# A pair sum moved ahead of the first product, a bank swapped, a transpose moved behind an addition, and a copy cut in two, in the first unit of a fused attention and feed-forward kernel

## The chip, the cores and the metric

The kernel runs on one core of one Trainium2 chip. The metric is the device time of one execution in microseconds (us); lower is better. The core's engines work side by side, each through its own list of instructions in order: TensorE (PE in the profile, with its weight loads as PEld), VectorE (DVE), ScalarE (ACT), GpSimd (POOL) and SyncE (SP), which issues most of the DMA transfers. They wait for each other on semaphores. What an engine's instruction waits for holds up everything behind it on that engine.

## The reference

Attention over keys and values that are averaged in groups of 8 rows, for 8 batches of 8 heads, 576 rows of 64; then a feed-forward layer with a sine activation on the 4608 rows of 512:

```python
k_p = k.reshape(B, H, Sp, pool, D).mean(axis=3)          # Sp = 576 / 8 = 72
v_p = v.reshape(B, H, Sp, pool, D).mean(axis=3)
scores = scale * np.matmul(q, k_p.transpose(0, 1, 3, 2))
attn = np.exp(scores - np.max(scores, axis=-1, keepdims=True))
attn = attn / (np.sum(attn, axis=-1, keepdims=True) + 1e-09)
attn_out = np.matmul(attn, v_p)
x = attn_out.transpose(0, 2, 1, 3).reshape(B * S, H * D)
h = x @ w_in                                             # 512 -> 2048
s = np.sin(alpha * h)
g = h + s * s / (alpha + 1e-09)
out = g @ w_out                                          # 2048 -> 512
```

All inputs and the output are float32.

## The kernel before

The feed-forward part is the bulk of the work on PE. Rows are taken in units of 512 (`self.NU` = 9 units). Both large products use a scheme with seven block products in the place of eight: sums and differences of blocks of `w_in` (`combine_w_in`, L678) and of `x` (`sums_of_x`, L803) go into seven products, and their results are combined in PSUM and on DVE. PE's time in the first half is the first of these products (`product` in `hidden`, L841), in the second half the second (L1321).

`hidden(u)` (L813) walks through 28 slots for a unit: four groups J of 256 columns, and in each group seven slots, one per product, in the order 1, 5, 6, 2, 7, 3, 4. Around the products it puts the copies between PSUM banks on ACT (`copy`, L817), the additions on DVE (`add`, L816; L1043), and the sines and squares on ACT (L991, L998). The attention of the next batch is cut into pieces that `carry(u)` (L1162) hangs into these slots: `at(slot, f, ...)` appends a piece, and the pieces of a slot are issued by `extras()` in the order in which they were appended. `product` in a slot comes after the slot's extras. So the order on each engine is written out by hand; no scheduler moves anything.

Batch 0 has no unit before it to hide in. `first_batch` (L1068) runs its attention at the start as far as is needed for the first product, and the rest of it lies in the first slots of unit 0: the pair sum of v for the second half of the heads (`sum_v_rows`, L203: matmuls L210 with a matrix of ones and zeros, copied by ACT at L211), the last 64 queries (`rest_q`, L401: transposes L406, copy L407), the transposes of the weights of heads 4 to 7 (`a_head(1)`, L467: L473 and L481), their products with v (`values`, L557: L563, L565; then ACT's L534 into `x` and DVE's differences L574), and the scores of the last 64 rows (`score(4)`: L348, then L355 and L356 on DVE).

PSUM has eight banks. The products of `hidden` rotate through banks 0 to 4 (`bank`), attention pieces through 5 to 7 (`abank`, which steps `self.aturn`), or they name a bank (`psum(shape, i)`). In `first_batch` the last call, `A.values((0, 1), (5, 6), 2, 0)`, leaves its results in banks 5 and 6; ACT reads them into `x` (L534, in four pieces), then DVE reads them for the differences (L574). Product 1 of group 0 needs the first two pieces of L534.

For batch 1, `load_q(1)` brings q into the tile `q0` by rows and heads. `pairs_q` (L87, copies L97 on ACT, one per tile of rows, five in all) reorders it into the tile `q1`. Then `q_t` (L279) transposes `q1` on PE (L287) and writes the turned q into a tile that is again `q0` (L288; DVE for tiles 0 and 1, ACT for 2 to 4): the tile that the raw q occupies. `k_t` (L271) does the same with the pooled keys (L276 on PE, L277 on DVE). `two_scores(0)` in slot 5 takes both (L315 on PE, shifts L338 and L339 on DVE).

The softmax weights of batch 1 follow in slots 9 to 19: `exp` on ACT (L364), `norm` (L370, L371 on DVE, L372 on POOL), `turn(i)` (32x32 transposes on DVE, L498 and L501 to L508) and `move` (DMA, L518), for four tiles i. `turn(2)` is in slot 17, `turn(3)` in slot 19. Slot 19 begins with the DVE addition L816 that reads the bank of product 7, and product 4 in slot 20 adds into that bank.

Of the kernel before, what the change touches and what calls it, by code (L numbers as in the profile page):

```python
# [19 lines left out]
P = 128  # L20
# [20 lines left out]
class Kernel:  # L41
# [214 lines left out]
    def attention(self, b):  # L256

        nc, D, H, Sp, NP, S = self.nc, self.D, self.H, self.Sp, self.NP, self.S
# [142 lines left out]
        def rest_q():  # L401

            rest = self.q_rest
            ps = self.abank([P, NP, 64])
            for hp in range(NP):
                nc.tensor.transpose(ps[:, hp], rest[:, 2 * hp:2 * hp + 2, :].rearrange("p h d -> p (h d)"), self.ident[:64, :64])  # L406
            nc.scalar.copy(out=self.qt_tiles(b)[:, 4, :, :64], in_=ps)  # L407
# [189 lines left out]
        def all_values():  # L597
# [26 lines left out]
            for hp in hps:  # L624
                to_x(ps[hp].rearrange("p (t j) -> p j t", t=4), hp, 0, 512)
            to_x(rest, slice(0, 4), 512, 64)

        return SimpleNamespace(**{f.__name__: f for f in (k_t, q_t, products, score, two_scores, two_shifts, exp, norm, new_a, turn, move, values, values_rest, all_values,
                                                          k_head, k_last, q_head, rest_q, products_head, soft_shift, soft_exp, norm_head, norm_rest, a_head, a_rest)})


# [436 lines left out]
    def first_batch(self):  # L1068

        nc = self.nc  # L1070
        self.att = [self.attention(b) for b in range(self.B)]
        A = self.att[0]

        far = [self.home(i, [P, 4 * POOL * self.D]) for i in (1, 2)]
        h = [self.hp.tile([P, 4 * POOL * self.D], F32, name="h") for _ in range(2)]
        self.k_rows = far[0][:].rearrange("p (h t d) -> p h t d", h=self.H, t=4)
        self.k_sums = far[1][:, 0:1024].rearrange("p (h u d) -> p h u d", h=self.H, u=2)
        self.new_q(0)
        self.load_alpha(self.hp.tile([P, P], F32, name="s", bufs=1)[:])
        self.load_q_heads(0, 0, 2, nc.scalar)  # L1080
        add_k = [self.load_k_heads(0, nc.sync, nc.vector)]
        add_rest = self.load_k_rest(h[1][:, 576:832], far[1][:, 1024:1152])
        one = self.sm.tile([P, 1], F32, name="one")
        nc.scalar.activation(out=one[:], in_=self.ident[:, 0:1], func=AF.Sqrt)

        def fill(n):

            for _ in range(n):
                nc.tensor.matmul(self.psum([P, 4, P], 4), self.full[:], self.full[:].unsqueeze(1).to_broadcast([P, 4, P]), start=True, stop=True)
        fill(5)  # L1090
        self.turn_alpha()
        refine = self.root()
        nc.scalar.activation(out=one[:], in_=one[:], func=AF.Exp)
        add_k[0]()
        tr = self.new_tr()
        nc.gpsimd.memset(tr[:, 2048:], 0.0)
        self.a0 = tr[:, 0:2048].rearrange("p (t j s k) -> p t j s k", t=4, j=4, s=2)
        self.z0 = tr[:, 2048:2560].rearrange("p (t hp x k) -> p t hp x k", t=4, hp=4, x=4)
        self.kb2 = h[1][:, 0:self.H * self.Sp].rearrange("p (h k) -> p h k", h=self.H)
        self.a4 = self.last[:64, 0:512].rearrange("p (j s k) -> p j s k", j=4, s=2)  # L1100
        self.z4 = self.last[:64, 512:640].rearrange("p (hp x k) -> p hp x k", hp=4, x=4)
        nc.gpsimd.memset(self.z4, 0.0)
        for hp in range(1, 4):
            add_k.append(self.load_k_heads(hp, nc.sync, nc.vector if hp < 2 else nc.gpsimd))
            if hp < 3:
                self.load_q_heads(0, 2 * hp, 2 * hp + 2)
        self.load_v_rows(0, h[0][:], self.tp.tile([P, self.DM], F32, name="p5")[:])
        self.load_q_heads(0, 6, 8)
        self.load_w_in()
        self.load_w_in_part(0)  # L1110
        self.q_rest = self.A[3][:64, 0, 512:1024].rearrange("p (h d) -> p h d", h=self.H)
        A.new_a()
        fill(4)
        A.k_head(0)
        add_rest()
        A.q_head(0)
        A.k_last()
        for f in add_k[1:]:
            f()
        fill(1)  # L1120
        A.products_head(0)
        A.q_head(1)
        A.k_head(1)
        A.soft_shift(0)
        A.soft_exp(0)
        fill(1)
        A.products_head(1)
        A.k_head(2)
        A.q_head(2)
        A.soft_shift(1)  # L1130
        A.soft_exp(1)
        A.norm_head(0, nc.gpsimd)
        A.norm_head(1, nc.vector)
        fill(2)
        A.products_head(2)
        self.sum_v_rest(0, 0)
        self.sum_v_rows(0, 0, 3)
        A.k_head(3)
        A.q_head(3)
        A.soft_shift(2)  # L1140
        A.a_head(0, (1, 7, 0), (0,))
        self.add_v_rows(1)
        self.combine_w_in(0, (0,), nc.gpsimd)
        A.products_head(3)
        A.a_head(0, (1, 7, 0), (1,))
        A.soft_exp(2)
        A.soft_shift(3)
        A.norm_head(2, nc.gpsimd)
        A.soft_exp(3)
        A.norm_head(3, nc.vector)  # L1150
        A.values((0, 1), (5, 6), 2, 0)
        self.combine_w_in(0, (1,))
        self.combine_w_in(0, (2, 3), nc.gpsimd)
        self.refine = refine
        self.load_q_rest(0, self.q_rest)
        for e in range(2):
            self.load_k(1, e)
            self.pool_k[e]()
        self.load_q(1)
        self.load_w_in_part(1)  # L1160

    def carry(self, u):  # L1162
# [3 lines left out]
        at = lambda slot, f, *a: x[slot].append(lambda: f(*a))  # L1166
        last = self.B - 1
        b = u + 1
        if u == 0:
            A0, A = self.att[:2]  # L1170
            at(1, self.sum_v_rows, 0, 1, 2, 1)
            at(1, A0.rest_q)
            at(1, A0.a_head, 1, (5, 7, 2))
            at(1, self.refine)
            at(2, A0.values, (2, 3), (2, 1), 1, 1)
            at(2, A0.score, 4)
            at(2, self.sums_of_x, 0, 2)
            at(2, self.sums_of_x, 0, 3)
            at(2, self.load_w_in_part, 2)
            at(2, self.load_w_in_part, 3)  # L1180
            at(2, self.pairs_q, 1, range(5))
            at(4, self.combine_w_in, 1, (0, 1, 2, 3), self.nc.gpsimd)
            at(4, A.q_t, 0, self.nc.vector.tensor_copy)
            at(4, A.q_t, 1, self.nc.vector.tensor_copy)
            at(4, A.k_t)
            at(7, self.load_v, 1)
            at(7, lambda: self.pool_v())
            for i in range(2):
                at((5, 10)[i], A.two_scores, i)
            at(13, A.two_shifts)  # L1190
            for i in range(2, 5):
                at(5 + i, A.q_t, i)
            at(9, A0.exp, 4)
            for i in range(4):
                at((9, 9, 15, 15)[i], A.exp, i)
                at((10, 10, 16, 16)[i], A.norm, i)
                at((13, 13, 17, 19)[i], A.turn, i)
            at(8, self.combine_w_in, 2, (0, 1, 2, 3), self.nc.gpsimd)
            at(13, A0.norm_rest)
            at(17, self.combine_w_in, 3, (0, 1), self.nc.gpsimd)  # L1200
            at(17, self.combine_w_in, 3, (2, 3), self.nc.gpsimd)
            at(23, A0.a_rest)
            at(24, lambda: A0.values_rest((5, 6, 7, (self.turn + 1) % 5)))
            for r in (32, 96):
                at(3, self.nc.gpsimd.memset, self.aM[r:r + 32, :, 704:736], 0.0)
            at(19, A.move, range(3))
            at(20, A.move, (3,), nc.scalar, (0,))
            at(21, A.move, (3,), nc.scalar, (1,))
            at(26, A.all_values)
            at(9, self.load_q, 2)  # L1210
            at(23, self.inner_w_in)
            for e in range(2):
                at(12, self.load_k, 2, e)
                at(17, lambda e=e: self.pool_k[e]())
            at(27, self.att[2].k_t)
            turn = 23
        else:
            at(0, self.sums_of_x, u, 2)
            at(0, self.sums_of_x, u, 3)
        if 0 < u < last:  # L1220
            A = self.att[b]
# [366 lines left out]
```

## Time and profile before

| | |
|---|---|
| median of 3 runs | 905.33 us (903.86 to 905.96) |
| the profiled execution | 904.85 us |
| its span, first to last instruction | 903.1 us |
| PE busy | 894.6 us, 99% |
| DVE busy | 678.1 us, 75% |
| ACT busy | 448.4 us, 50% |
| POOL busy | 211.2 us, 23% |
| mean granted PE clock | 1.00 |

The page gives the busy time of each engine over the span. The view of waits says which engine, at which line, waited for which: total, number of times, longest. The view in order of time has, per row, start, busy time, engine, line, operation, tiles written and read, shapes and count; in brackets the engine's idle time just before and what ended it. Rows are merged where equal instructions follow each other, so the busy time of a row with x8 is that of eight. Matmuls overlap by a little, so a row's end reaches slightly into the next row. A float32 matmul shows as two or more records.

Where the first slots lie on PE, in us from the start of the span: product 1 of group 0 at 19.91, product 5 at 24.23, product 6 at 28.78, product 2 at 30.61, product 7 at 33.46, the first scores of batch 1 at 35.31, product 3 at 36.47. Group 2 has product 3 at 64.22 and product 4 at 67.10.

### The profile page before, as it was taken

The page shows a single profiled execution, that of the slowest core. Times are in us where ns is not written, and L with a number is a line of the kernel's source. Part 1 is how long each engine was busy: PE and PEld are TensorE (multiplying, and loading weights), DVE is VectorE, ACT ScalarE, POOL GpSimd, SP SyncE. Part 2 cuts the span into 40 slices and gives each one's busy share as a digit, 9 for nine tenths or more (in the row PEclk, how much of TensorE's full clock was granted, in tenths as well). Part 3 has the DMA queues.
Part 4 walks back from the last instruction along what each step waited for, and adds up shares of the span by engine and source line. Part 5 has one row for each costly group of instructions (what it writes and reads, how often), then busy time and mean ns, then how long its engine had stood idle before and what let it go on. Part 6 is the DMA issues. An engine that isn't in the chain of part 4 may idle for free.

```text
span 903.1 us, 17918 instructions
## 1 busy us (share of the span) xinstructions
PE 894.6 (99%) x7002; PEld 815.2 (90%) x7002; DVE 678.1 (75%) x1012; ACT 448.4 (50%) x1072; POOL 211.2 (23%) x216
## 2 busy tenths in 40 slices
PE   8999999999999999999999999999999999999998
PEld 5787888888888888888888999999999999999998
DVE  7685766768577685764557799979798888889895
ACT  5686776877768778687976611111111111111111
POOL 5688552824437253430000000000000000000000
PEclk9999999999999999999999999999999999999999
DMA  9965857759477595648217346261618162533401
GB/s 264 245 199 152 231 153 200 194 155 270 136 214 186 174 235 138 180 143 297 93 68 231 99 139 205 52 200 39 224 27 229 35 193 71 172 92 122 142 14 40
DMA packets 128746, 141.12 MB, mean 156 GB/s; under 512 B 46920, under 2 KB 95704, under 8 KB 128664
## 3 DMA queue, kind: packets, MB, share of 16 engines
q1 hardware_dynamic: 125880, 137.88, 53.3%
q10 hardware_dynamic: 2784, 2.11, 0.9%
q8 instruction: 55, 0.90, 0.4%
q14 instruction: 27, 0.22, 0.1%
HBM read 75.37 MB, written 47.19 MB: 136 GB/s over the span
## 4 chain that ended last, share of the span: by engine, by line
PE 91%; DMA 3%; DVE 2%; SPq 2%; POOL 2%; issue 0%; ACT 0%; DVEq 0%; POOLq 0%
PE PS L841 42%; PE PS L1321 41%; PE PS L1021 3%; PE PS L315 2%; PE PS L607 2%; DMA a<-in_moe_w_in_dram 2%; DMA kvin<-in_v_dram 1%; SPq L676 1%; PE PS L620 1%; DVE x L1276 1%; POOL kvin L131 0%; POOL as L682 0%; DVE s L1276 0%; POOL ex L372 0%; SPq L84 0%
## 5 line engine op out<-in xcount | busy, mean ns | idle before, releaser
L841 PE MATMUL PS<-home,a 128*128 128x256 f32 x1104 | 257.9, 381 | 1.6 <-DVE h L816 1.0
L841 PEld LDWEIGHTS PS<-home,a 128*128 128x128 f32 x1104 | 205.2, 190 | 34.9 <-issue 5.0
L841 PE MATMUL PS<-home,as 128*128 128x256 f32 x768 | 183.0, 382 | 0.0
L841 PEld LDWEIGHTS PS<-home,as 128*128 128x128 f32 x768 | 141.6, 190 | 19.8 <-ACT PS L817 1.2
L1371 POOL TENSOR_TENSOR cc<-cc,cb 128x576 f32<-128x576 f32 x1 | 2.0, 1976 | 501.8 <-DVE cb L1276 501.8
L1321 PE MATMUL PS<-s,wb 128*128 128x144 f32 x896 | 119.1, 286 | 0.0
L1321 PEld LDWEIGHTS PS<-s,wb 128*128 128x128 f32 x896 | 113.7, 190 | 0.1
L998 ACT ACTIVATE s<-s,c 128x256 f32<-128x256 f32 (+1 forms) x228 | 113.5, 564 | 0.0
L816 DVE TENSOR_TENSOR h<-PS,p 128x512 f32<-128x512 f32 x72 | 49.2, 683 | 63.0 <-PE PS L841 36.6
L131 POOL TENSOR_TENSOR kvin<-kvin 96x768 f32<-96x768 f32 (+3 forms) x42 | 74.3, 1769 | 73.0 <-DMA kvin<-in_v_dram 71.4
L1449 ACT COPY PS<-PS 128x144 f32<-128x144 f32 x56 | 14.7, 263 | 144.8 <-PE PS L1321 138.1
L991 ACT ACTIVATE s<-h,al 128x256 f32<-128x256 f32 x144 | 65.6, 510 | 40.2 <-DVE h L816 39.4
L1321 PE MATMUL PS<-r,wb 128*128 128x144 f32 x512 | 73.3, 286 | 0.3 <-DVE r L1276 0.3
L1321 PE MATMUL PS<-s,a 128*128 128x144 f32 x512 | 73.2, 286 | 0.0
L1043 DVE TENSOR_TENSOR h<-PS,s 128x512 f32<-128x512 f32 x36 | 24.7, 685 | 59.8 <-ACT s L998 59.8
L991 ACT ACTIVATE s<-PS,al 128x256 f32<-128x256 f32 x144 | 60.0, 469 | 18.3 <-PE PS L841 17.4
L1321 PEld LDWEIGHTS PS<-r,wb 128*128 128x128 f32 x512 | 67.1, 190 | 0.5 <-DVE r L1276 0.5
L1321 PEld LDWEIGHTS PS<-s,a 128*128 128x128 f32 x512 | 67.0, 190 | 0.0
L817 ACT COPY PS<-PS 128x512 f32<-128x512 f32 x72 | 41.5, 576 | 35.4 <-PE PS L841 30.8
L1469 ACT COPY PS<-PS 128x144 f32<-128x144 f32 x56 | 14.7, 263 | 88.1 <-PE PS L1321 88.1
L1321 PE MATMUL PS<-x,wb 128*128 128x144 f32 x384 | 54.9, 286 | 0.0
L1321 PE MATMUL PS<-s,we 128*128 128x144 f32 x384 | 54.9, 286 | 0.0
(216 smaller groups left out, 1405.6 us busy)
## 6 DMA issues: line engine op xcount, KB each, us to landing
g_bridge<-h SPq DMA_DIRECT2D x72, 512.0 KB
r<-g_bridge SPq DMA_DIRECT2D x31, 1152.0 KB
out_dram<-o SPq DMA_DIRECT2D x122, 72.0 KB
kvin<-in_k_dram SPq DMA_DIRECT2D x14, 576.0 KB
q<-in_q_dram SPq DMA_DIRECT2D x7, 1024.0 KB
kvin<-in_v_dram SPq DMA_DIRECT2D x14, 512.0 KB
aM<-tr SPq DMA_DIRECT2D x54, 92.0 KB
aM<-tr SPq DMA_DIRECT2D x54, 88.0 KB
```

Source lines behind the costliest of these rows:

```text
L131: self.nc.gpsimd.tensor_tensor(out=t[..., 0:w] if w > D else out, in0=t[..., 0:w], in1=t[..., w:2 * w], op=OP.add)
L315: nc.tensor.matmul(ps[e][r0 + r:r0 + r + q.shape[-1], h, :], q[s], kb[s, hp, :], start=True, stop=True)
L607: nc.tensor.matmul(o[r:r + 64], w, x, start=start and i < 2, stop=False, skip_group_check=True)
L816: add = lambda o, x, y: nc.vector.tensor_tensor(out=o, in0=x, in1=y, op=OP.add)
L817: copy = lambda o, x: nc.scalar.copy(out=o, in_=x)
L841: nc.tensor.matmul(ps[:, jj, :], self.A[p][:, kk, f * P:(f + 1) * P], x[:, kk, :], start=(start and n == 0), stop=(kk == 1), skip_group_ch ...
L991: self.nc.scalar.activation(out=G.s[:, i, jj, j, :], in_=src[:, jj], func=AF.Sin, scale=self.al[:, f:f + 1])
L998: self.nc.scalar.activation(out=x, in_=x, func=AF.Square, scale=self.c[:, f:f + 1])
L1021: nc.tensor.matmul(o, W[m][:, G.J - J0], X[m], start=start and n == 0, stop=True, skip_group_check=True)
L1043: add = lambda o, x, y: self.nc.vector.tensor_tensor(out=o, in0=x, in1=y, op=OP.add)
L1321: nc.tensor.matmul(out, W[:, J // 2, J % 2, :], A[:, J, :], start=(start and J == 0), stop=(J == self.NJ - 1), skip_group_check=True)
L1449: nc.scalar.copy(out=x1[:, 0, :], in_=x0[:, 1, :])
```

## The change

Five edits, all in batch 0's end and unit 0:

- `sum_v_rows(0, 1, 2, 1)` is issued at the end of `first_batch`, right behind `values((0, 1), ...)`, and so ahead of product 1 of group 0, in the place of slot 1, where it stood behind that product. On ACT its copy L211 comes ahead of the copy behind product 1.
- `rest_q` takes bank 7 in the place of the next of the rotation, which was bank 6 here. `self.aturn` is still stepped, so the banks of all later pieces stay as they were.
- `a_head(1)` has its second main transposes in bank 6 in the place of bank 7.
- `pairs_q(1)` is issued in two parts: tiles 0 and 1 in slot 2 as before, tiles 2, 3 and 4 at the head of slot 4. On ACT the three copies then come behind the two copies of slot 3 (L817), a load of the activation table, and the first sines and squares of slot 4.
- `turn(2)` moves from slot 17 to slot 19, ahead of `turn(3)`. On DVE it then comes behind the addition L816 that opens slot 19.

On POOL and SP the order is unchanged. Line numbers of the changed kernel are one or two higher from L404 on.

```diff
@@ rest_q
             rest = self.q_rest
-            ps = self.abank([P, NP, 64])
+            self.aturn += 1
+            ps = self.psum([P, NP, 64], 7)
@@ first_batch
         A.values((0, 1), (5, 6), 2, 0)
+        self.sum_v_rows(0, 1, 2, 1)
         self.combine_w_in(0, (1,))
@@ carry, u == 0
-            at(1, self.sum_v_rows, 0, 1, 2, 1)
             at(1, A0.rest_q)
-            at(1, A0.a_head, 1, (5, 7, 2))
+            at(1, A0.a_head, 1, (5, 6, 2))
@@
-            at(2, self.pairs_q, 1, range(5))
+            at(2, self.pairs_q, 1, (0, 1))
+            at(4, self.pairs_q, 1, (2, 3, 4))
             at(4, self.combine_w_in, 1, (0, 1, 2, 3), self.nc.gpsimd)
             at(4, A.q_t, 0, self.nc.vector.tensor_copy)
@@
-                at((13, 13, 17, 19)[i], A.turn, i)
+                at((13, 13, 19, 19)[i], A.turn, i)
```

## The prediction

> **What bounds the kernel now.** I read the busy times first, then what TensorE (PE) waited for, then the order of time in the first 70 us, where every moved step lies.
>
> ```profile
> PE 894.6 (99%) x7002; PEld 815.2 (90%) x7002; DVE 678.1 (75%) x1012; ACT 448.4 (50%) x1072; POOL 211.2 (23%) x216
> ```
> ```profile
> PE PS L841 <- DVE h L816: 1.0, 1, 1.0
> PE PS L841 <- ACT home L534: 0.5, 1, 0.5
> PE PS L406 <- DVE home L574: 0.2, 1, 0.2
> ```
>
> PE is the bound: 8.5 us of the 903.1 are idle. Of its waits, these three lie beside the change and hold 1.7 us together; after 67.10 us the waits on PE hold only one more, of 0.3 us. The chain that ended last is PE from 67.10 us on, but for a detour of 14 us through ACT and DVE at 524 us that starts and ends on PE. So what PE loses or gains by 67.10 is what the kernel loses or gains. Next, the order of time where PE first waits:
>
> ```profile
> 18.32 1.13 PE L565 MATMUL PS<-aM,vz 32*128 32x512 f32 x4
> 19.91 1.99 PE L841 MATMUL PS<-home,a 128*128 128x256 f32 x8 [0.47 <-ACT home L534]
> 21.68 0.74 DVE L574 SCALAR_TENSOR_TENSOR home<-PS,home 128x256 f32<-128x256 f32 x2
> 21.83 0.44 PE L210 MATMUL PS<-h,twos 128*64 128x128 f32 x4
> 22.48 0.46 PE L406 MATMUL PS<-ident,as 64*128 64x64 f32 x4 [0.21 <-DVE home L574]
> 22.87 1.09 PE L473 MATMUL PS<-ident,tr 128*128 128x128 f32 x8
> ```
>
> The pair sum (L210) stands behind the first main product (19.91), which itself waits; the last queries (L406) wait until DVE has read bank 6 (22.42). Then the copies of q:
>
> ```profile
> 28.76 1.09 ACT L534 ACTIVATE home<-PS 128x512 f32<-128x512 f32 x2 [3.75 <-DVE home L574]
> 29.73 2.69 ACT L97 COPY q<-q 128x512 f32<-128x512 f32 x5
> 32.32 0.58 ACT L817 COPY PS<-PS 128x512 f32<-128x512 f32 x1
> 33.03 1.29 DVE L288 COPY q<-PS 128x512 f32<-128x512 f32 x2 [0.31 <-ACT PS L817]
> 33.44 1.28 ACT L991 ACT_TABLE_LOAD   x1
> 33.46 1.92 PE L841 MATMUL PS<-home,a 128*128 128x256 f32 x8
> 34.24 0.55 DVE L277 COPY kblk<-PS 128x288 f32<-128x288 f32 x1
> 34.73 0.84 ACT L991 ACTIVATE s<-PS,al 128x256 f32<-128x256 f32 x2
> 35.31 1.23 PE L315 MATMUL PS<-kblk,q 64*64 64x72 f32 x64
> ```
>
> ACT is busy without a break from 28.76 to 37.16. PE passes from product 7 (33.46) to the scores (L315, 35.31) without a wait: DVE had the turned q (L288) and k (L277) ready at 34.79, half a microsecond early. Last, the only wait of PE near 1 us:
>
> ```profile
> 64.22 1.89 PE L841 MATMUL PS<-home,as 128*128 128x256 f32 x8
> 65.56 0.71 DVE L498 STREAM_TRANSPOSE tr<-ex 128x512 f32<-128x512 f32 x1
> 66.39 0.65 DVE L816 TENSOR_TENSOR h<-PS,p 128x512 f32<-128x512 f32 x1
> 67.10 3.72 PE L841 MATMUL PS<-home,a 128*128 128x256 f32 x16 [0.99 <-DVE h L816]
> ```
>
> PE is ready at 66.11, but product 4 adds into the bank that L816 must read, and on DVE that addition stands behind the third transpose of weights, which waited for POOL.
>
> **The change, part by part.** Times are those of the profile before; a shift is against it.
>
> *Pair sum first.* L210 moves to where PE idles: from 19.44 (end of L565) to 19.91. Sixteen of these took 1.02 us to the next start at 13.01, so four take 0.26 and fit. Its inputs are there: the POOL additions (L201) ended at 16.81 and DVE last read bank 2 at 18.50. On ACT its copy (0.27) passes the copy behind product 1, in ACT's 1.25 us gap before 21.94: nothing.
>
> *Bank 7 for the last queries.* L406 no longer waits for DVE; the transposes L473 behind it now do, bank by bank (5, free at about 22.05; then 6, free at 22.42). PE: product 1 from 19.91 as before, L406 at 21.83, L473 at 21.83 + 0.39 = 22.22, its second half at 22.66, both behind the releases. Against 22.87 that is 0.65 us gained by the two edits together. It carries on: L473 copies, product 5, values, L348, product 6 follow PE, and the DVE work between has 0.61 us of idle (before L574 at 28.30) and begins earlier too. ACT's L534 comes at 28.76 - 0.65 = 28.11. Bounds: nothing (if L473's new waits are late) to 0.68 (both idle times); I take 0.65, as each step is a row.
>
> *q copied in two parts.* This is the dear one. The turned q of batch 1 is written (L288) into the tile q0, which the raw q of batch 1 occupies: the raw heads 0 and 1 lie where turned tile 0 goes, with all their rows. So the first L288 on DVE needs all five copies L97. Before, the fifth ended at 32.42, ahead of L288 at 33.03. Now three stand on ACT behind the sines and squares. From 28.11 on ACT's order gives: L97 twice from 28.11 + 0.97 = 29.08, pitch 0.52 (five in 2.59); L817 at 30.16, when product 6 ends (28.13 + 1.99 = 30.12); second L817 at 30.68; table load 0.60 later, 31.28; sines 1.29 later, 32.57 (product 2 is done at 31.85); squares 0.73 later, 33.30; 0.80 later, 34.10, the three copies, the last ending 34.10 + 2 x 0.52 + 0.63 = 35.77. DVE's L288 starts at 35.83 against 33.03; L277 1.21 later, at 37.04, ends 37.59; PE's scores start at 37.65.
>
> Queued behind the waiting L288 on DVE are the second L288, L277, the addition L816 and all the shifts of the scores; PE waits for L277, ACT's next sines for L816 (at 38.2 instead of 36.17, a smaller shift than PE's). PE itself comes at 35.31 - 0.65 = 34.66, so it stands for 2.99 us, and the scores are 37.65 - 35.31 = 2.34 us later than before. L817 comes 2.16 us earlier, which buys nothing: PE wasn't waiting for it (no idle at 33.46). On SP the load of the next q (44.98) waits for PE's L287 and shifts with it, with the store and the load of k behind it (48.29, 49.29); these are needed some 25 us later. POOL's order and inputs there don't hang on PE.
>
> *Third transpose behind the addition.* From 37.65 to 66.11 PE's work was without idle, so it is ready for product 4 at 66.11 + 2.34 = 68.45. DVE: the shifts of 54.92 now end at about 59.4; turned weights 0 and 1 (POOL done at 58.66 and 59.77) need no more waiting, and the row of work that ended at 65.43 ends some 0.55 later, at 65.98. Then L816 waits for product 7 (64.2 + 2.34 = 66.55) and ends at 67.2: ahead of 68.45. The wait of 0.99 is gone: minus 0.99. What is late next: third transpose 67.3, fourth 68.2 (before 67.24), so L816/ACT moves/SP moves come about 1 us later than before; PE needs them 1.35 later. Product 6 of the last group (72.93) then needs ACT's copy (71.72 + 1.0 + 0.58 = 73.3) at 74.3. All hidden; without that cover at most 1 us.
>
> *Sum:* -0.65 + 2.99 - 0.99 = +1.35 us. On the profiled execution (904.85 us: span 903.1 and 1.75 around it) that is 906.2. The median of the runs, 905.33, is 0.48 above that execution; on it the forecast is 906.7, which I give.
>
> Two costs no row shows. DVE's copies beside POOL's additions: they lay beside the same additions (32.76 to 37.84) before, at the durations used, but a DVE operation of 0.23 us took 1.73 at 24.87 beside POOL's L131, so 0 to 1.5 us; I take 0, the row of the same pair of operations. And PE after a stand of 3 us. The stand of 0.99 was followed by a granted clock of 1.00. At the end of the program the last matmul ends at 898.76, and the view by windows has a clock of 1.00 up to 902.0 and then these rows (length, busy time on five engines, granted clock, DMA share, GB/s):
>
> ```profile
> 902.00:902.50 0.50, 0.00 (x0) 0.00 (x0) 0.00 (x0) 0.00 (x0) 0.00 (x0) 0.86 0.00 0
> 902.50:903.10 0.60, 0.00 (x0) 0.00 (x0) 0.00 (x0) 0.00 (x0) 0.00 (x0) 0.50 0.00 0
> ```
>
> 0.86 is 0.14 us of the 0.50 at half, so the clock fell at 902.36, after 3.6 us of standing. 2.99 is nearer to that than to 0.99, but short of it. I take 0. If it falls: the first matmuls of the program (L1089) start 0.43 us apart from 1.06 to 4.36 and 0.21 apart at 11.16 (the clock column reads 1.00 for both; I go by the pitch); the one at 6.93 (0.38 us long against 0.57) is already quick. So half speed would last 3.3 to 5.9 us and cost half of it, 1.7 to 2.9.
>
> **The rivals.**
>
> *A. The stand is short or absent (not slower).* Place: L288 on DVE. Even is reached if the last L97 ends 1.35 earlier, by 34.42; without a stand PE comes to product 4 at 65.46, waits for L816 until 66.1, and product 6 of the last group is then held by ACT's copy to 72.3, so 0.6 us are gained: 904.3 on the profiled execution, 904.7 on the median. For it: DVE had 0.5 us of slack and the copies are short. Against it: five reads of one tile must end before its first overwriting, and ACT's row from 28.76 has no gap to give.
>
> *B. The early gain doesn't come.* If PE reaches L473 at 22.87 as before (DVE's L574 late), everything on ACT shifts back with it and the scores start at 38.30: +2.99 - 0.99 = +2.0, 907.3 on the median. For it: L473 still needs both L574, 0.2 us ahead by my count. Against: L574's place on DVE is unchanged.
>
> *C. The clock falls in the stand.* +1.35 + 1.7 to 2.9 = +3.0 to +4.3: 908.4 to 909.6. For it: 3 us of standing is near 3.6; against: it is less, and the wait begins right behind dense matmuls. The Trainium skill (TensorE: Matmul & The Clock Gate, "Why this matters for your kernels") wants no PE gaps above about 3 us between bursts, and its Part 1 puts the window at 3.4 us, free-running. By that rule the stand of this change would just pass or just fall; the tail's 3.6 us agrees with the longer figure.
>
> *D. DVE and POOL collide* at 35.8 to 37.6: up to +1.5 more, 908.2.
>
> **How the numbers follow.** A measurement of this kernel tells about 0.2% (1.8 us) from no change: above 907.1 is slower, below 903.5 faster. The forecast (+0.7 to +2.0, 906.0 to 907.3) has 0.60, of which 0.24 falls above the bound, with the scatter of medians (runs from 903.9 to 906.0), and 0.02 below the other. A has 0.12 (0.04 of it faster), B 0.12 (0.08 slower), C 0.08 and D 0.08, both slower. Sums: slower 0.48, within 0.46, faster 0.06. The range goes from A's 904.3 to 909.2, inside C: about 1 in 10 left out on both sides, one more for scatter.
>
> **What would show it.** Right: PE's wait at the scores (L315, by DVE's L277) near 3.0 us at 34.7 to 37.7, three L97 at about 34.1 ending near 35.8, no wait before product 4 near 68.4, L210 between 19.4 and 19.9, L473 at about 22.2. Wrong: L288 on DVE before the last L97, a wait at the scores under 1.6 us, a clock under 1.00 behind 37.7, or a new wait of PE between 68 and 75.

## The result, and the profile after

The changed kernel takes 908.62 us in the median (905.98 to 911.38, 18 executions), the kernel before 905.38 beside it (903.86 to 906.79, 18 executions). The ratio is 1.0033, with a 95% interval of 1.0024 to 1.0042: 3.0 us slower, 2.2 to 3.8. The forecast was 906.7 us, and its sum +1.35.

The profiled execution of the changed kernel took 905.98 us (span 904.2) against 904.85 before: only +1.1. So the profile shows the forecast's sum, and it does not show the other 2 us. Here is what PE waited for in it (the view of waits: total, number of times, longest):

```profile
PE PS L315 <- DVE kblk L277: 2.5, 1, 2.5
PE PS L1090 <- DVE full L1485: 1.1, 1, 1.1
PE PS L387 <- DVE home L164: 0.5, 1, 0.5
PE PS L1323 <- DVE r L1278: 0.3, 1, 0.3
```

The three waits of before beside the change (1.0, 0.5 and 0.2) are gone, and one wait of 2.5 us has come: the scores of batch 1 wait for the turned keys. The other three are those at the start and near the end that the kernel before has too. The order of time shows how it arises:

```profile
19.25 0.44 PE L210 MATMUL PS<-h,twos 128*64 128x128 f32 x4
19.79 1.99 PE L842 MATMUL PS<-home,a 128*128 128x256 f32 x8
21.71 0.46 PE L407 MATMUL PS<-ident,as 64*128 64x64 f32 x4
22.10 1.09 PE L474 MATMUL PS<-ident,tr 128*128 128x128 f32 x8
...
31.19 1.28 ACT L992 ACT_TABLE_LOAD   x1
32.75 0.28 PEld L276 LDWEIGHTS PS<-ident,kp 96*128 96x128 f32 x3 [0.38 <-POOL kp L131]
33.06 1.92 PE L842 MATMUL PS<-home,a 128*128 128x256 f32 x8
34.01 1.65 ACT L97 COPY q<-q 128x512 f32<-128x512 f32 x3
35.69 1.29 DVE L288 COPY q<-PS 128x512 f32<-128x512 f32 x2 [4.51 <-ACT q L97]
36.90 0.53 DVE L277 COPY kblk<-PS 128x288 f32<-128x288 f32 x1
37.49 1.23 PE L315 MATMUL PS<-kblk,q 64*64 64x72 f32 x64 [2.51 <-DVE kblk L277]
```

The pair sum (L210) and the last queries (L407) go through without a wait. The three late copies of q (L97) end at 35.66, DVE begins to overwrite the raw q at 35.69, and the scores start at 37.49, 2.51 us after PE ended product 7 at 34.98. Further on, product 4 of group 2 begins without a wait:

```profile
66.40 1.89 PE L842 MATMUL PS<-home,as 128*128 128x256 f32 x8
66.66 0.69 DVE L817 TENSOR_TENSOR h<-PS,p 128x512 f32<-128x512 f32 x1 [1.09 <-PE PS L842]
67.27 0.70 DVE L499 STREAM_TRANSPOSE tr<-ex 128x512 f32<-128x512 f32 x1
68.13 3.62 PE L842 MATMUL PS<-home,a 128*128 128x256 f32 x16
```

The start of product 1 differs between profiled executions, from 19.8 to 22.1 us, so distances from it are compared below. From product 1 to product 4 of group 2 it is 47.19 us before and 48.34 after; on to the first scores of the next batch in unit 1 it is 72.29 and 73.49. So +1.2 us is lost on this stretch, and with it the +1.1 of the profiled execution is accounted for.

What the other executions lose goes with their mean granted clock. In 14 of the 18 executions of the changed kernel it is 0.998 or less (median time 908.8, 3.5 us above the kernel before), and in only 6 of 59 of the kernel before, timed with the experiments below. In the 4 of the changed kernel where it is 0.999 or more the times are 905.98, 906.5, 906.5 and 906.96, in the mean 906.5, that is +1.1 again. The profiled execution is one of these four.

### The profile page after: what moved, and what is told of

The parts are those of the page before. It is cut to its first block, busy times and chain, and to the rows that moved or that the text cites. A ratio compares the mean times of both kernels' runs of the same rounds, so it can differ in the third digit from the quotient of the medians.

```text
span 904.2 us, 17920 instructions
## 1 busy us (share of the span) xinstructions
PE 894.7 (99%) x7002; PEld 815.3 (90%) x7002; DVE 677.6 (75%) x1012; ACT 448.6 (50%) x1072; POOL 212.1 (23%) x216
## 3 DMA queue, kind: packets, MB, share of 16 engines
HBM read 75.37 MB, written 47.19 MB: 136 GB/s over the span
## 4 chain that ended last, share of the span: by engine, by line
PE 95%; DVE 2%; SPq 1%; ACT 1%; DMA 1%; issue 0%; DVEq 0%
PE PS L842 44%; PE PS L1323 41%; PE PS L1022 3%; PE PS L315 2%; PE PS L608 2%; SPq L677 1%; PE PS L621 1%; DVE x L1278 1%; DMA a<-in_moe_w_in_dram 1%; PE PS L1090 0%; DVE s L1278 0%; DVE r L1278 0%; PE PS L420 0%; PE PS L276 0%; SPq L101 0%
## 5 line engine op out<-in xcount | busy, mean ns | idle before, releaser
L842 PEld LDWEIGHTS PS<-home,as 128*128 128x128 f32 x768 | 141.6, 190 | 19.8 <-ACT PS L818 1.2
L817 DVE TENSOR_TENSOR h<-PS,p 128x512 f32<-128x512 f32 x72 | 49.1, 683 | 64.4 <-PE PS L842 38.1
L131 POOL TENSOR_TENSOR kvin<-kvin 96x768 f32<-96x768 f32 (+3 forms) x42 | 74.6, 1776 | 71.4 <-DMA kvin<-in_v_dram 69.7
L818 ACT COPY PS<-PS 128x512 f32<-128x512 f32 x72 | 41.4, 576 | 35.1 <-PE PS L842 30.3
```

The costliest lines, as they stand in the source:

```text
L131: self.nc.gpsimd.tensor_tensor(out=t[..., 0:w] if w > D else out, in0=t[..., 0:w], in1=t[..., w:2 * w], op=OP.add)
L817: add = lambda o, x, y: nc.vector.tensor_tensor(out=o, in0=x, in1=y, op=OP.add)
L818: copy = lambda o, x: nc.scalar.copy(out=o, in_=x)
L842: nc.tensor.matmul(ps[:, jj, :], self.A[p][:, kk, f * P:(f + 1) * P], x[:, kk, :], start=(start and n == 0), stop=(kk == 1), skip_group_ch ...
```

## The experiments

Two theories stood against each other. The first (1, or T1): the loss is the stand at the scores as PE's order shows it, +1.1 to +1.35 us, and the rest of the 3 us is something else, not tied to the stand. The second (2, or T2): in most executions the granted clock falls in or behind the stand, and that is the rest. The kernels were timed beside the kernel before: the first four of them (`filled`, `split_alone`, `whole_copy`, `split_3_2`) against 905.68 us (25 executions), the next four against 905.81 (34), `early_alone` against 905.59 (13).

**The stand filled with idle work** (`filled`). Ten matmuls whose result nobody reads, put into the changed kernel where PE stands:

```diff
+            def fill():
+                for _ in range(10):
+                    self.nc.tensor.matmul(self.psum([P, 4, P], 2), self.full[:], self.full[:].unsqueeze(1).to_broadcast([P, 4, P]), start=True, stop=True)
+            at(5, fill)
             for i in range(2):
                 at((5, 10)[i], A.two_scores, i)
```

> The changed kernel with ten matmuls of 128x512 (bf16 ones, into bank 2, which nothing reads) between product 7 and the first scores of batch 1, where TensorE stands for 2.5 us. They take about 10 x 0.21 = 2.1 us at full clock and end before the scores are released. Theory 1 (the stand costs its own length and nothing else, and the rest of the measured 3.2 us comes from elsewhere): the stand seems filled but the scores start at 37.5 all the same, and the median stays where that of the changed kernel is, about +3.2 us over the kernel before. Theory 2 (in most executions the clock of TensorE falls in the stand and takes some us to come back): granted clock 1.000 in every execution, median at +1.1 to +1.4 us, scatter as narrow as that of the kernel before.

Measured: 906.85 us (906.09 to 908.17, 11 executions), ratio 1.0013 (1.0004 to 1.0021), so +1.2 us. The mean clock was 0.999 or 1.000 in all 11. In the order of time:

```profile
35.70 2.32 PE L1192 MATMUL PS<-full 128*128 128x512 bf16 x10
38.63 1.23 PE L315 MATMUL PS<-kblk,q 64*64 64x72 f32 x64 [0.61 <-DVE kblk L277]
```

The scores come no earlier: they still wait for the keys, 0.61 us behind the last idle matmul. In this execution they start 18.35 us behind product 1, against 17.70 in the first profile of the changed kernel; part of that delay shows ahead of the filling, where the transposes L474 wait 0.35 us for DVE's L575 and ACT's L97 waits 0.21 us for the load of q. PE gains no work done, and yet 1.8 us of the 3.0 are back. So the stand costs two things: its own length, and a lower clock behind it when PE is left idle. The second theory holds: the time is what it expected, and the clocks nearly so.

**The changed kernel once more** (`again`), for an execution in which the clock falls.

> The changed kernel once more, for a look at one more execution. If the clock falls in or right behind the stand in most executions (14 of 18 so far had a mean clock of 0.998 or less), then with 3 chances in 4 the granted clock reads 0.50 for 3.4 us from a point between 2.4 us after the start of the stand and 1 us behind its end, and the execution takes 2.5 to 4 us more than the kernel before; otherwise the clock stays at 1.00 there and it takes about 1.1 more.

It took 909.56 us (span 907.8, mean clock 0.996). By windows (stretch, length, busy time of PE, PEld, DVE, ACT and POOL, granted clock, DMA share, GB/s):

```profile
37.50:39.00 1.50, 0.00 (x0) 0.00 (x0) 1.12 (x2) 0.34 (x1) 1.50 (x2) 1.00 1.14 300
39.00:39.50 0.50, 0.00 (x0) 0.00 (x0) 0.50 (x3) 0.00 (x0) 0.50 (x2) 0.97 1.10 178
39.50:40.00 0.50, 0.33 (x12) 0.33 (x16) 0.50 (x2) 0.00 (x0) 0.50 (x1) 0.50 1.16 176
40.00:42.50 2.50, 2.50 (x66) 2.27 (x59) 1.63 (x5) 0.91 (x2) 0.54 (x1) 0.50 1.05 186
42.50:43.00 0.50, 0.50 (x3) 0.41 (x2) 0.50 (x2) 0.00 (x0) 0.00 (x0) 0.61 1.05 213
43.00:44.00 1.00, 1.00 (x7) 0.87 (x6) 0.97 (x2) 0.00 (x0) 0.00 (x0) 1.00 0.89 199
```

and the scores in the order of time:

```profile
39.67 2.20 PE L315 MATMUL PS<-kblk,q 64*64 64x72 f32 x64 [2.51 <-DVE kblk L277]
41.80 2.51 PE L842 MATMUL PS<-home,as 128*128 128x256 f32 x8
```

PE stood from 37.16 to 39.67, the same 2.51 us as in the first profile. A clock of 0.97 over 0.5 us is 0.03 us at half, so the clock fell at about 39.47; 0.61 is 0.39 us at half, so it rose at about 42.89: some 3.41 us at exactly 0.50. The scores take 2.20 us in place of 1.23. From product 1 to the scores of unit 1 it is 74.97 us, against 73.49 in the execution without the fall: 1.48 us for this fall. This execution had a second fall, from 8.76 to about 12.17 us, where no edit lies; it comes behind a wait of 1.3 us, and product 1 is late with it (21.97 against 19.79). Against the profile before, product 1 comes 2.06 us later and the way from it to the scores of unit 1 is 2.68 us longer, 4.74 together; the two executions differ by 4.71 us (909.56 against 904.85). So in this execution the start, the stand and the fall account for all of the loss.

**Only the copies of q cut** (`split_alone`), in the kernel before:

```diff
-            at(2, self.pairs_q, 1, range(5))
+            at(2, self.pairs_q, 1, (0, 1))
+            at(4, self.pairs_q, 1, (2, 3, 4))
```

> The kernel before with only the copy of q cut in two. Both theories: TensorE comes to the scores at 35.31 and stands until about 38.3, 3.0 us, and the old wait of 0.99 before product 4 is gone although the third transpose was not moved, since TensorE now comes late enough: +2.0 us by theory 1. By theory 2 a longer stand lets the clock fall at least as often as in the changed kernel: +4 us, clocks of 0.996 to 0.998.

Measured: 909.09 us (907.63 to 910.36, 5 executions), ratio 1.0036 (1.0023 to 1.005), +3.3 us. That lies between the two numbers, nearer to that of the second theory. PE's longest wait:

```profile
PE PS L315 <- DVE kblk L277: 2.9, 1, 2.9
```

The mean clock was 1.000, 0.998, 0.998, 0.996 and 0.996. In the profiled one the clock fell at 39.76, that is 0.7 us after the stand (36.17 to 39.04) had ended and with PE busy again, and stayed at 0.50 for 3.41 us. This edit alone is enough for the whole loss. It also showed something that speaks against a step of the forecast: product 4 did not wait, although `turn(2)` was not moved.

**The copies in one piece** (`whole_copy`), in the changed kernel:

```diff
-            at(2, self.pairs_q, 1, (0, 1))
-            at(4, self.pairs_q, 1, (2, 3, 4))
+            at(2, self.pairs_q, 1, range(5))
```

> The changed kernel with the copy of q whole again, all five in slot 2; the other edits stay. Both theories: no stand before the scores, the wait before product 4 at most 0.1 us, 0.6 to 1.0 us faster than the kernel before, clock 1.000. A rival, that one of the other edits costs something: slower than before or level with it.

Measured: 905.9 us (904.45 to 907.77, 12 executions), ratio 1.0002 (0.9993 to 1.0011). The loss is gone, and with it the stand, but the gain that was expected of the other edits isn't there in the times. In the profile the way from product 1 to the scores of batch 1 is 0.26 us shorter than before (15.14), that to product 4 1.42 us shorter (45.77), and to the scores of unit 1 still 0.95 shorter (71.34); part of it goes to a wait of 0.3 us for ACT's copy of the turned last queries (L591 for L491). The profiled execution gave its gain away at the start: its clock was at 0.50 from 7.98 to 11.39, and product 1 came at 22.09. That the times are level with the kernel before isn't explained by this: 2 of the 12 have a mean clock of 0.998 or less.

**Cut behind the third tile** (`split_3_2`):

```diff
-            at(2, self.pairs_q, 1, (0, 1))
-            at(4, self.pairs_q, 1, (2, 3, 4))
+            at(2, self.pairs_q, 1, (0, 1, 2))
+            at(4, self.pairs_q, 1, (3, 4))
```

> The changed kernel with the copies cut three and two in the place of two and three. The last copy ends 0.5 us earlier, so the stand is about 2.0 us. Theory 1: 0.5 us faster than the changed kernel, +2.7 us if its 3.2 have another cause. Theory 2: +0.6 us plus what the clock costs; if a stand of 2.0 us is too short for it to fall, clock 1.000 and a median of +0.6; if it falls as often, +2.6.

Measured: 907.92 us (906.17 to 908.58, 7 executions), ratio 1.0019 (1.0007 to 1.003), +1.7 us. The stand was 2.72 us, not 2.0: the expectation missed. ACT has no gap here, so the third copy, put ahead of the two copies L818, the table load and the sines, pushes all of these back by its 0.52 us, and the last copy ends where it did: 7.61 us behind the start of L535, against 7.67 in the changed kernel. Here only the place of the last copy in ACT's order counts, not how many lie ahead. The transposes L474 also waited 0.50 us for DVE's L575 in this execution, so PE and ACT are both later behind product 1 than in the changed kernel. Of the 7 executions 2 had a mean clock of 0.998 or less, a smaller share than with the stand of 2.5 us; two at 0.999 took 907.92 and 908.58, so the mean clock does not mark every long execution. In the profiled one the clock fell 2.4 us after the stand began and stayed at 0.50 for 3.41 us.

**The second part one slot earlier** (`split_slot_3`): still two parts, with L818 between them, but ahead of the table load and the sines.

```diff
             at(2, self.pairs_q, 1, (0, 1))
-            at(4, self.pairs_q, 1, (2, 3, 4))
+            at(3, self.pairs_q, 1, (2, 3, 4))
```

> The changed kernel with the second part of the q copies in slot 3 in the place of slot 4: still two parts, but ahead of the table load, the sines and the squares on ScalarE. If the place behind the sines makes the stand, and not the cutting: the last copy ends about 3 us earlier, by 32.9, TensorE does not stand before the scores (under 0.3 us), the way from product 1 of group 0 to product 4 of group 2 is 0.8 to 1.4 us shorter than in the kernel before (47.2), clock 0.999 to 1.000 in nearly all executions, median 0 to 1.0 us under the kernel before. If cutting the copy in two costs something by itself: a stand of 2 us or more and slower than before.

Measured: 905.65 us (903.95 to 907.44, 12 executions), ratio 0.9999 (0.9989 to 1.0009). In the order of time:

```profile
33.16 1.66 ACT L97 COPY q<-q 128x512 f32<-128x512 f32 x3
34.84 1.28 ACT L992 ACT_TABLE_LOAD   x1
34.85 1.29 DVE L288 COPY q<-PS 128x512 f32<-128x512 f32 x2 [1.57 <-ACT q L97]
...
37.02 1.08 PEld L315 LDWEIGHTS PS<-kblk,q 64*64 64x64 f32 x64 [0.33 <-issue]
```

The scores wait for nobody ("issue" names no releaser). 1 of 12 executions has a mean clock of 0.998 or less: the profiled one, whose clock was at 0.50 from 8.50 to 11.91, at the start, behind a wait of 1.3 us. Later PE waits 0.46 us for ACT's copy L818 at product 6 of the last group, as in `turn_alone` below. So it isn't the cutting that costs, but the place behind table load, sines and squares, about 2.8 us of ACT.

**A shorter filling** (`filled_4`): four idle matmuls in place of ten.

```diff
-                for _ in range(10):
+                for _ in range(4):
```

> Four matmuls of 128x512 in the place of ten in the stand: 0.85 us of work, 1.6 us of standing left. If the clock goes by the share of standing in a window of 3.4 us, 1.6 is under the half and it holds in most executions: +1.1 to 1.5 us, clocks 0.999 to 1.000. If a gap of 1.6 us is enough: +2 to +3.2 us, clocks 0.996 to 0.998.

Measured: 908.29 us (906.3 to 911.2, 12 executions), ratio 1.003 (1.0018 to 1.0042), +2.5 us. PE stands for the rest:

```profile
PE PS L315 <- DVE kblk L277: 1.7, 1, 1.7
```

In 5 of the 12 the mean clock is 0.998 or less. So by the clocks a gap of 1.7 us is short enough in some executions and not in others, though no fall was seen in place: the profiled execution has none. The expectation that four matmuls keep the clock failed. Five falls in twelve at some 1.6 us each are 0.7 us in the mean, with the 1.1 of the stand 1.8: that is within the interval (1.6 to 3.8), but at its lower end, and what else may add to it was not found.

**The third transpose back in its place** (`turn_undone`), in the changed kernel:

```diff
-                at((13, 13, 19, 19)[i], A.turn, i)
+                at((13, 13, 17, 19)[i], A.turn, i)
```

> The changed kernel with the third transpose of weights back in slot 17, ahead of the addition. The sum of the forecast took 0.99 us off for that move. If the move earns it, this kernel waits about 1 us before product 4 of group 2 and is 1 us slower than the changed kernel, +4.2 us. If the late TensorE alone makes the wait go (as the kernel with only the split copy lets expect), there is no wait above 0.2 us and the time is that of the changed kernel, +3.2 us.

Measured: 908.04 us (905.82 to 909.18, 10 executions), ratio 1.0023 (1.0012 to 1.0035), +2.2 us. The stand is 2.5 us as in the changed kernel, there is no wait at product 4, and from product 1 to product 4 it is 48.34 us, the same to the hundredth. The moved transpose gained nothing in the changed kernel: PE comes so late that DVE's addition is in time in either order. The clock was at 0.998 in 6 of the 10.

**The third transpose alone** (`turn_alone`): the same line the other way round, in the kernel before.

```diff
-                at((13, 13, 17, 19)[i], A.turn, i)
+                at((13, 13, 19, 19)[i], A.turn, i)
```

> The kernel before with only the third transpose behind the addition. The wait of 0.99 before product 4 goes; what is left of it is given back in part when ScalarE's copies behind the fourth transpose come no earlier. 0.3 to 1.0 us faster than the kernel before, which the interval of this measurement (about 0.8 us to each side) may not tell from level; in the profile no wait before product 4, and the way from product 1 of group 0 to product 4 of group 2 shorter by 0.9 to 1.0 us than 47.2. If another wait takes its place: that way unchanged.

Measured: 905.58 us (904.78 to 907.15, 12 executions), ratio 0.9996 (0.9986 to 1.0007): level. The order of time shows that the 0.99 us are gained at product 4 and then lost again:

```profile
66.17 3.72 PE L841 MATMUL PS<-home,a 128*128 128x256 f32 x16
68.70 1.50 ACTq L518 DMA_DIRECT2D aM<-tr  x2
...
72.08 0.57 ACT L817 COPY PS<-PS 128x512 f32<-128x512 f32 x1 [0.20 <-PE PS L489]
...
72.80 1.97 PE L841 MATMUL PS<-home,as 128*128 128x256 f32 x8 [0.73 <-ACT PS L817]
```

From product 1 to product 4 it is 46.20 us (47.19 before), but then PE waits 0.73 us for ACT's copy, and further on 0.3 us for another (L590 for L490); at the scores of unit 1 it is 72.56, 0.27 behind the kernel before.

**The early edits alone** (`early_alone`): pair sum and the two banks in the kernel before; the copies of q whole and `turn(2)` in slot 17.

```diff
+            self.aturn += 1
+            ps = self.psum([P, NP, 64], 7)
...
+        self.sum_v_rows(0, 1, 2, 1)
...
-            at(1, self.sum_v_rows, 0, 1, 2, 1)
-            at(1, A0.a_head, 1, (5, 7, 2))
+            at(1, A0.a_head, 1, (5, 6, 2))
```

> The kernel before with the pair sum ahead of product 1 and the banks swapped, the two other edits undone. TensorE comes to the scores 0.65 us earlier, reckoned from product 1 of group 0 (14.75 in the place of 15.40), with no stand there. If the addition before product 4 of group 2 is held by the transpose and POOL, the wait there grows from 0.99 to about 1.6 us and the way from product 1 to product 4 stays at 47.2: level with the kernel before. If the gain carries through: 46.5, and 0.6 us faster.

Measured: 906.04 us (904.14 to 907.42, 10 executions), ratio 1.0005 (0.9994 to 1.0017): level. The scores of batch 1 come without a stand, but 15.13 us behind product 1 and not 14.75: that expectation missed. Product 4 comes 46.17 us behind product 1, 1.02 shorter than before, and the scores of unit 1 at 71.29, 1.00 shorter. The wait before product 4 is only 0.24 us:

```profile
66.37 3.72 PE L842 MATMUL PS<-home,a 128*128 128x256 f32 x16 [0.24 <-DVE h L817]
```

This is not the gain of the edits carried through. The addition stands behind DVE's third transpose, which began at 64.84 here and at 65.56 before; it waits for softmax weights from POOL, and POOL's work up to there begins with the load of v (first line before, second here):

```profile
44.82 4.57 POOL L131 TENSOR_TENSOR kvin<-kvin 128x1024 f32<-128x1024 f32 x2 [6.98 <-DMA kvin<-in_v_dram]
44.08 4.58 POOL L131 TENSOR_TENSOR kvin<-kvin 128x1024 f32<-128x1024 f32 x2 [5.29 <-DMA kvin<-in_v_dram]
```

Product 4 starts 22.28 us behind this in the profile before and 22.29 here. So in both the load of v sets product 4, and not PE; in the profile before, the chain that ended last runs this way too. POOL began 0.74 us earlier in the span here, and product 1 came 0.29 later. Whether the edits brought the load forward was not separated; in the two profiles of the changed kernel POOL begins on v at 44.83 and 46.72. So the 0.99 us of the profile before depends on when v lands. Why the 1.0 us of this profile is not found in the times stays open.

The way from product 1, side by side (us; one profiled execution of each):

| kernel | to product 4 | to the scores of unit 1 | times against before | clock 0.998 or less |
|---|---|---|---|---|
| before | 47.19 | 72.29 | | 6 of 59 |
| changed | 48.34 | 73.49 | +3.0 | 14 of 18 |
| `again` (with the fall) | 49.83 | 74.97 | | |
| `filled` | 48.99 | 74.16 | +1.2 | 0 of 11 |
| `filled_4` | 48.35 | 73.55 | +2.5 | 5 of 12 |
| `turn_undone` | 48.34 | 73.18 | +2.2 | 6 of 10 |
| `split_alone` (with a fall) | 50.42 | 75.25 | +3.3 | 4 of 5 |
| `split_3_2` (with a fall) | 50.48 | 75.63 | +1.7 | 2 of 7 |
| `whole_copy` | 45.77 | 71.34 | +0.2 | 2 of 12 |
| `split_slot_3` | 45.76 | 71.75 | -0.2 | 1 of 12 |
| `turn_alone` | 46.20 | 72.56 | -0.2 | 0 of 12 |
| `early_alone` | 46.17 | 71.29 | +0.5 | 1 of 10 |

In the column of times, the first six kernels that were changed and timed differ from the one before by more than their intervals; the last four don't. No kernel was found that beats the one before. Behind the first scores of unit 1 the profiles hardly differ: from there to the start of PE's last row it is 805.4 to 805.5 us in eleven of the twelve, and 805.7 in `split_alone`. The table leaves out the start up to product 1, and one profile can be off its kernel's times: `filled` is 1.8 to 1.9 us longer than before in the table and 1.2 in the times.

## Why the prediction was right or wrong, step by step

*Pair sum and banks, -0.65.* Right in place and size: the transposes (L474) came 2.31 us behind product 1, against 2.96 before and 2.31 in the forecast, and the last L97 ended at 35.66 for 35.77. PE itself did not get all of it. The transposes of k (L276) waited 0.38 us for POOL, whose pooling of k (L131) took 4.06 us against 2.89 before (first line before, second after); the forecast had let POOL out there.

```profile
28.29 2.89 POOL L131 TENSOR_TENSOR kvin<-kvin 96x768 f32<-96x768 f32 x2
27.98 4.06 POOL L131 TENSOR_TENSOR kvin<-kvin 96x768 f32<-96x768 f32 x2
```

This is no accident of one execution. In eight of the nine profiles with the early edits this pooling takes 3.86 to 4.08 us and the weight loads of L276 wait 0.38 to 0.40 for POOL; in the three without them it takes 2.88 to 2.89 and nothing waits. In those eight DVE's two additions L812 come earlier, into the time of the pooling, and take 0.67 and 0.68 us where they took 1.05 and 1.08; in the ninth (`split_3_2`) the pooling takes 3.22 and the second addition 1.48. So it is likely that the two slow each other, but no run tests it. In the changed kernel it cost nothing, because PE then stood anyway; in `early_alone` and `whole_copy` it leaves 0.26 to 0.27 us of the 0.65 at the scores. The new wait of the transposes for DVE, which the forecast held possible, came too in two profiles: 0.35 us in `filled`, 0.50 in `split_3_2`. One price was too low: the four matmuls of the pair sum took 0.54 us up to the start of product 1, not 0.26; they just fitted into the gap.

*The late copies of q, +2.99.* The mechanism was right: PE stood for DVE's L277, DVE for the last L97, and L97 for the sines. The stand was 2.51, not 2.99, because PE came 0.32 us later (34.98 for 34.66) and the scores 0.16 earlier (37.49 for 37.65). The scores' shift behind product 1 is set by ACT and DVE and not by PE, and there the forecast was close: 2.30 us (17.70 against 15.40) for 2.34. `split_alone` shows that this edit alone makes the loss, and `split_slot_3` that the place behind the sines does.

*The third transpose, -0.99.* The wait did go, but not through the move: `turn_undone` has no such wait either. PE's own lateness removed it. What the forecast called hidden, "at most 1 us" at ACT's copy, is what `turn_alone` shows as soon as PE isn't late: 0.73 and 0.3 us of waits on ACT give the gain back. So the step was booked under the wrong edit; the sum stayed right. In the profile before the wait belongs to a chain that does not run through PE, from the load of v over POOL and DVE to the addition (`early_alone`); any lateness of PE above 0.99 us hides it.

*The sum, +1.35.* The profiled execution has +1.1, the four executions with an undisturbed clock +1.1, and the kernel with the stand filled +1.2. The sum is near for the work itself; the measured +3.0 is not this sum.

*"And PE after a stand of 3 us ... I take 0."* This is the step that failed: a term put at 0 that came to some 2 us. The forecast measured the stand against the 3.6 us after which the clock fell at the end of the program, and took what is below as safe. The clock does not wait for a stand of a given length: it fell 2.3 us after the start of a stand of 2.5 (`again`), 2.4 after that of one of 2.72 (`split_3_2`), and after the end of one of 2.87 (`split_alone`), and it did not fall in the first profile of the changed kernel, with the same 2.51. So the 3.6 us of the tail was one sample of something that varies, and not a threshold. The rule of the Trainium skill (TensorE: Matmul & The Clock Gate, Part 1), a free-running window of about 3.4 us, agrees with the 3.41 us of every fall that was read and with their varying start; its demand that a whole window be idle does not agree with falls in or behind waits of 1.3 to 2.9 us. What it is that the clock goes by within such a window was not settled.

*Rival C* was what happened, and it was given 0.08. The forecast itself, 906.7 with 906.0 to 907.3 around it, missed the measured 908.62; the wide range, 904.3 to 909.2, holds it only because it reached into C. Its price, 1.7 to 2.9 us at half speed for 3.3 to 5.9 us, was near: a fall is 3.41 us at half, 1.7 us less what lies in the stand, 1.48 in `again`. Its time, 908.4 to 909.6, holds the measured 908.62. In the changed kernel the executions with a low clock are 2.3 us above the others (median 908.8 against 906.5), 0.8 us more than the 1.48 of the one fall. Second falls at the start, which no edit touches, are part of that (`again` had one, and the two executions at 0.996 are 909.91 and 911.38); that they are all of it is not shown.

*A, B and D* did not happen: the stand was there, the transposes came when forecast, and DVE's two L288 took 1.29 us and L277 0.53 beside POOL, against 1.29 and 0.55 before. POOL and DVE did get into each other's time, but earlier, at the pooling of k, where PE lost 0.38 us.

## What to carry to other kernels

When an edit makes TensorE stand for 2.5 us or more in the midst of dense work, add the price of a clock fall as a likely case (here 3.41 us at half speed, 1.5 us in one trace and at most 1.7 by the length; 26 of 40 executions of the four kernels with stands of 2.5 to 2.9 us had a mean clock of 0.998 or less), and look at the granted clock of every execution and not of the profiled one alone. On an engine without gaps the place of the last copy in its order decides when it ends: cutting the group of copies cost nothing here, putting a part behind a table load and sines did. A wait that is removed is a gain only if the next engine is in time, and an earlier engine gains nothing where the wait hangs on a load; look who is second, and first try whether the wait is still there once the other edits are in.

## What was not expected of the hardware

- A stand of 2.5 us, well under the 3.6 us at the end of the program, is enough for the clock to fall, in some executions and not in others: 14 of 18 have a low mean clock. A low mean clock was also found in 5 of 12 with 1.7 us left at the scores, and falls were read at the start of the program behind waits of 1.3 us (`again`, `split_slot_3`) and 1.5 us (`whole_copy`).
- The fall may come when PE is busy again (`split_alone`: 0.7 us behind the stand), and dense work does not end it early: the six falls that were read, in five kernels, lasted 3.41 us at 0.50.
- Idle matmuls keep the clock: ten of them, 2.32 us, in all 11 executions, and that kernel is 1.8 us better than the one that stands. By the mean clock, four did not keep it in 5 of 12.
